# Linear attention and gated FFN on one core: the second batch's queries are loaded first, and later loads wait for transposes

## The chip, the cores and the metric

The kernel runs on one core of one Trainium2 chip, alone. The metric is the device time of one execution in microseconds. The kernel before took 594.44 us (median of 3 runs, 594.08 to 594.91). A core has five engines with a program each: TensorE (PE, matmuls), VectorE (DVE), ScalarE (ACT), GpSimd (POOL) and SyncE (SP). They meet only in semaphores. Here POOL issues all loads with a change of type, and SP issues the stores and the DMA transposes. The data itself is moved by 16 DMA engines, which both queues share.

## The reference

Eight batches of eight heads, 1024 positions, 64 numbers a head. Keys and values are projected along the positions to 64 rows, then comes softmax attention, then a feed-forward network with a sigmoid gate on all 8192 rows.

```python
k_proj = einsum('ks,bhsd->bhkd', E, k);  v_proj = einsum('ks,bhsd->bhkd', F, v)
attn = softmax(q @ k_proj^T / 8)               # over the 64 projected rows
x = (attn @ v_proj) as (8192, 512)             # heads side by side
out = (sigmoid(x @ w_gate) * (x @ w_val)) @ w_out      # 512 -> 1536 -> 512
```

Inputs and outputs are float32; the loads turn the inputs into bfloat16.

## The kernel before, in words

*Order.* Every instruction is entered in one list by hand (`add`), with the names of what it reads and writes. From the names the waits are worked out; each engine then runs its own instructions in the order of the list. A load or a transpose that waits therefore holds up what stands behind it on POOL or SP.

*Work.* A batch has two blocks of 512 rows. For a block, 12 slices of the hidden layer (`msteps`, slice m = 0 to 11) are computed: four matmuls each for gate and value, then the gate on ACT and DVE. Behind them come four output tiles of 128 rows (`oproj`, tt = 0 to 3), 12 matmuls each with the output weights wO, an evacuation by DVE into one of four buffers `ost` and a store from SP. The output tiles of a block stand among the slices of the following block. The list `todo` holds slices and tiles of a batch, numbered from 0; `gaps` says behind which slice a tile comes. For the first batch `todo` has 27 entries: 0 to 10 are block 0 (its first entry holds two slices), the rest block 1 with the tiles of block 0.

*Attention of the next batch.* Its steps are put between those entries (`put(i, fn)`: behind entry i; `spots` for the ten steps): `kv` projects keys and values (K first, then V), `turn_k` turns the keys, `sc(0)` and `sc(1)` compute the scores of heads 0 to 3 and 4 to 7, `den` and `split` compute the divisors (four reciprocals and two more operations on DVE), `bc(0)` and `bc(1)` broadcast them, `xo(0)` and `xo(1)` apply the values and write the FFN's input `xT`. The scores need queries with the head's 64 numbers on the partitions. For batch 0 TensorE turns them. From batch 1 on SP issues four DMA transposes of two heads each (`transpose_q`, r = 0 to 3, called r0 to r3), from the buffer `Qb` to `qT`. By the names that they write, r1 waits for r0 and r3 for r2. `sc(0)` reads r0 and r1, `sc(1)` r2 and r3.

*Loads.* K, V and Q of a batch are one load each. K and V go round three buffers `KV` (K of batch b in 2b mod 3, V in 2b+1 mod 3), Q has two. Called Kb, Vb and Qb with the batch's number, POOL's order before is: K0, half of Q0, V0, the gate and value weights and the other half of Q0 among them, K1, V1, Q1, then wO (which waits until Q1's transposes have finished), then K2, Q2, V2, K3, Q3, V3 and so on. A load waits until its buffer has been read. V2 goes where K1 was, V3 where K2 was: each V from batch 2 on waits for the `kv` of the batch before, and what stands behind it waits too.

*Transposes on SP.* Those of Q1 stand first behind the loads of E and F. Those of Q2 stand behind the store of output tile 0 of block 1, in batch 1. Those of batch b+2 stand at entry 20 of batch b, from b = 1 on.

Of the kernel before, what the change touches and what calls it, by code (L numbers as in the profile page):

```python
# [12 lines left out]
P = 128  # L13
# [14 lines left out]
class Plan:  # L28
# [9 lines left out]
    def add(self, eng, fn, r=(), w=(), x=(), dma=None):  # L38
        op = Op()
        op.eng, op.fn, op.dma, op.need = eng, fn, dma, False  # L40
        op.sem, op.val = None, 0
        deps = {}

        def dep(o, raw):
            if o is op:
                return
            if o.eng == eng and o.dma is None:
                if eng == "PE" or (eng != "POOL" and not raw):
                    return
            deps[id(o)] = o  # L50

        for k in r:
            for o in self.writers.get(k, ()):
                dep(o, True)
        for k in tuple(w) + tuple(x):
            for o in self.writers.get(k, ()):
                dep(o, False)
            for o in self.readers.get(k, ()):
                dep(o, False)
        for k in r:  # L60
            self.readers.setdefault(k, []).append(op)
        for k in tuple(w) + tuple(x):
            self.writers[k] = [op]
            self.readers[k] = []
        op.deps = list(deps.values())
        for o in op.deps:
            o.need = True
        if dma is not None:
            self.dma_count[dma] = self.dma_count.get(dma, 0) + 16
            op.sem, op.val = dma, self.dma_count[dma]  # L70
        self.ops.append(op)
        return op
# [46 lines left out]
def bass_linformer_attn__then__ffn_glu_sigmoid_kernel(  # L119
# [15 lines left out]
    NR = H // 2  # L135
    SCALE = 1.0 / (DH ** 0.5)

    with contextlib.ExitStack() as es:

        def sbuf(name, shape, dtype):  # L140
            return es.enter_context(nc.sbuf_tensor(name, shape, dtype))
# [31 lines left out]
        qT = [sbuf(f"qT{i}", [P, H, 512], BF16) for i in range(2)]  # L173
# [9 lines left out]
        wO = sbuf("wO", [P, NF, DM], BF16)  # L183
# [24 lines left out]
        def mm(b, o, lhsT, rhs, r, start=True, stop=True, tp=None, tr=False):  # L208
            kw = {}
            if tp is not None:  # L210
                kw["tile_position"] = tp
            if tr:
                kw["is_transpose"] = True
            else:
                kw["start"], kw["stop"] = start, stop
            return add("PE", lambda e: e.matmul(o, lhsT, rhs, **kw), r=r, x=[("bank", b)])  # L216
# [16 lines left out]
        def load(o, i, w, sem, r=()):  # L233
            add("POOL", lambda e: e.dma_start(o, i), r=r, w=w, dma=sem)  # L234

        def load_k(b):
            n = 2 * b % 3
            load(
                KV[n][:, :, :],
                k[b].rearrange("h (p t) d -> p h (t d)", t=NT),  # L240
                [("KV", n)],
                f"KV{n}",
            )

        def load_v(b):
            n = (2 * b + 1) % 3
            load(
                KV[n][:, :, :],
                v[b].rearrange("h (p t) d -> p h (t d)", t=NT),
                [("KV", n)],  # L250
                f"KV{n}",
            )

        def load_q(b):
            s = b % 2
            load(
                Qb[s][:, :, :],
                q[b].rearrange("h (p t) d -> p h (t d)", t=NT),
                [("Q", s, 0), ("Q", s, 1)],
                f"Q{s}",  # L260
            )
# [18 lines left out]
        def start_loads():  # L280
            for src, rows, n in ((E, slice(0, 64), "E"), (F, slice(64, 128), "F")):
# [4 lines left out]
                    dma="in" + n,  # L286
                )
            load_k(0)
            pool(lambda e: e.iota(col_i[:, :], [[1, P]], channel_multiplier=0), w=["col_i"])
            pool(lambda e: e.iota(row_i[:, :], [[1, 1]], channel_multiplier=1), w=["row_i"])  # L290
# [135 lines left out]
        def busy(n):  # L426
            for _ in range(n):
                mm(FB[3], bank[FB[3]][:, 0:P], ident[:, :], ident[:, :], ["ident"])
# [184 lines left out]
        def transpose_q(b):  # L613
            s = b % 2
            for r in range(NR):
                add(
                    "SP",
                    lambda e, r=r: e.dma_start_transpose(  # L618
                        qT[s][:, 2 * r : 2 * r + 2, :].rearrange("p h (t c) -> p (h t) c", c=P),
                        Qb[s][:, 2 * r : 2 * r + 2, :].rearrange("p h c -> p (h c)"),  # L620
                    ),
                    r=[("Q", s, 0), ("Q", s, 1)],
                    w=[("qT", s, r), ("qT", s, 0, r // 2), ("qT", s, 1, r // 2)],
                    dma=f"qT{s}{r}",
                )
# [130 lines left out]
        def msteps(blk, ms):  # L756
            s, hf = (blk // 2) % 2, blk % 2
            pbs = {}
            for m in ms:
                for n in "GV":  # L760
                    pbs[m, n] = ffn.next()
            for i in range(NI):
                for m in ms:
                    j = max(x for x in range(4) if WCH[x] <= m * P)
                    for n, W in (("G", wG), ("V", wV)):
                        if len(ms) > 1:
                            mm_one(blk, m, j, i, n, W, pbs[m, n], s, hf)
            if len(ms) == 1:
                m = ms[0]
                j = max(x for x in range(4) if WCH[x] <= m * P)  # L770
                for n, W in (("G", wG), ("V", wV)):
                    for i in range(NI):
                        mm_one(blk, m, j, i, n, W, pbs[m, n], s, hf)
            for m in ms:
                gate(blk, m, pbs[m, "G"], pbs[m, "V"])
# [81 lines left out]
        bc(1)  # L857
        xo(1)
        busy(10)
        load_k(1)  # L860
        load_v(1)
        load_q(1)

        def load_wo():
            load(
                wO[:, :, :],
                moe_w_out.rearrange("(m p) c -> p m c", p=P),
                ["wO"],
                "wO",
                r=[("qT", 1, r) for r in range(NR)],  # L870
            )

        for b in range(B):
            todo = []
            for blk in (2 * b, 2 * b + 1):
                ms = [[m] for m in range(NF)]
                if blk == 0:
                    ms = [[0, 1]] + ms[2:]
                if blk == 1:
                    gaps = {9: [0], 10: [1], 11: [2, 3]}  # L880
                else:
                    gaps = {2: [0], 5: [1], 8: [2], 11: [3]}
                for m in ms:
                    todo.append(lambda blk=blk, m=m: msteps(blk, m))
                    if blk >= 1:
                        for tt in gaps.get(m[-1], ()):
                            todo.append(lambda blk=blk, tt=tt: oproj(blk - 1, tt, ffn.next()))
            at = {}

            def put(i, fn):  # L890
                at.setdefault(i, []).append(fn)

            if b == 0:
                qt, sc, den, bc, xo = half_unit(1, att)
                put(1, lambda: (qt(0), qt(1)))
                put(2, lambda: sc(0))
                put(4, lambda: sc(1))
                put(5, den)
                put(7, lambda: (bc(0), xo(0)))
                put(9, lambda: (bc(1), xo(1)))  # L900
                spots = (14, 15, 17, 18, 19, 19, 21, 22, 23, 24)
            else:
                spots = (3, 6, 10, 13, 16, 16, 20, 23, 26, 29)
            if b + 1 < B:
                for i, fn in zip(spots, attention(b + 1)):
                    put(i, fn)
            def load_next(n):
                load_k(n)
                load_q(n)
                load_v(n)  # L910

            if b == 0:
                put(8, lambda: (transpose_q(1), load_wo()))
                put(22, lambda: load_next(2))
            else:
                if b == 1:
                    put(3, lambda: transpose_q(2))
                if b + 2 < B:
                    put(4, lambda b=b: load_next(b + 2))
                    put(20, lambda b=b: transpose_q(b + 2))  # L920
            for i, slot in enumerate(todo):
                slot()
                for fn in at.get(i, ()):
                    fn()
            assert max(at, default=0) < len(todo)
# [33 lines left out]
```

## Time and profile before

| | |
|---|---|
| median of 3 runs | 594.44 us |
| the profiled execution | 596.05 us, span 594.3 us |
| mean granted TensorE clock | 0.991 |
| PE busy | 563.1 us |
| DVE, ACT, POOL busy | 253.4, 200.8, 30.2 us |
| loads (queue q0), stores and transposes (queue q1) | 29.89 and 24.65 MB |

Times within the execution count from the start of the span. A row of a timeline or of the chain gives start and length in us, then engine, line and operation, then the tiles as written<-read with partitions and elements, and x with a count when several are merged. In brackets stands the idle time before it and what ended it. The granted clock is 1.00 at full speed and 0.50 at half. L216 is the line through which all matmuls are entered, L234 all loads, L618 the transposes, L681 to L691 the divisors. `pF` are the four PSUM banks of the FFN, `pA` those of attention. q0 and q1 are the DMA queues of POOL and SP.

### The profile page before, as it was taken

To read this page: it belongs to the slowest core of one execution; us is meant where nothing else is said; L and a number is where in the kernel's file an instruction comes from. 1 tells how busy PE (TensorE), PEld (TensorE's weight loads), DVE (VectorE), ACT (ScalarE), POOL (GpSimd) and SP (SyncE) were. 2 spreads that over 40 slices of the span, in tenths; PEclk is the share of its full clock that TensorE was granted. 3 is DMA by queue.
4 is the path that set the end of the run, shared out by engine and by line. 5 is a ranking of instruction groups with operands and counts; after the bars stand their busy time and mean duration, and the time that the engine had idled before them with its cause. 6 is when DMAs were issued, how large, how long until landed. Compare 5 with 4: busy or idle time off the path is not lost.

```text
span 594.3 us, 7808 instructions
## 1 busy us (share of the span) xinstructions
PE 563.1 (95%) x3150; PEld 255.5 (43%) x3206; DVE 253.4 (43%) x393; ACT 200.8 (34%) x371; POOL 30.2 (5%) x43
## 2 busy tenths in 40 slices
PE   5799859969999999999999999999999999999997
PEld 5444324424444444444444444444444444444443
DVE  2444425215363365433563364533654344633332
ACT  2454621323523533144423334234332434222220
POOL 8000300100001000010001000000000000000000
PEclk9999979989999999999999999999999999999999
DMA  9997699985405913095313904050331000000002
GB/s 155 202 206 134 93 203 233 165 135 107 106 37 97 169 54 88 19 169 114 72 54 69 206 29 106 36 104 21 54 88 37 19 35 36 18 36 36 35 36 88
DMA packets 70756, 55.04 MB, mean 93 GB/s; under 512 B 31168, under 2 KB 62400, under 8 KB 70720
## 3 DMA queue, kind: packets, MB, share of 16 engines
q0 software_dynamic: 31776, 29.89, 32.5%
q1 hardware_dynamic: 38944, 24.65, 15.6%
q8 instruction: 25, 0.41, 0.3%
q14 instruction: 11, 0.09, 0.0%
HBM read 60.29 MB, written 16.78 MB: 130 GB/s over the span
## 4 chain that ended last, share of the span: by engine, by line
PE 82%; DMA 16%; issue 1%; DVE 1%; SPq 0%; POOL 0%; POOLq 0%; DVEq 0%
PE pF L216 74%; PE pA L216 8%; DMA Qb<-in_q_dram 7%; DMA qT<-Qb 5%; DMA wO<-in_moe_w_out_dram 2%; DMA KV<-in_k_dram 2%; DVE xT L729 0%; DVE ost L822 0%; SPq L618 0%; POOL KV L234 0%; DVEq L102 0%; POOLq L102 0%; POOLq L944 0%; SPq L102 0%
## 5 line engine op out<-in xcount | busy, mean ns | idle before, releaser
L795 DVE SCALAR_TENSOR_TENSOR hT<-sig,pF 128x512 bf16<-128x512 f32 x192 | 131.2, 686 | 207.8 <-PE pF L216 135.2
L220 ACT ACTIVATE sig<-pF 128x512 f32<-128x512 f32 x192 | 115.3, 601 | 276.7 <-PE pF L216 269.2
L216 PE MATMUL pF<-xT,wG 128*128 128x512 bf16 x748 | 195.1, 380 | 2.3 <-issue 1.6
L216 PE MATMUL pF<-xT,wV 128*128 128x512 bf16 x748 | 195.1, 379 | 1.9 <-DVE xT L600 0.9
L216 PE MATMUL pF<-wO,hT 128*128 128x512 bf16 x705 | 165.9, 384 | 9.5 <-DMA wO<-in_moe_w_out_dram 8.0
L216 PEld LDWEIGHTS pF<-xT,wV 128*128 128x128 bf16 x768 | 75.1, 98 | 90.9 <-issue 0.6
L216 PEld LDWEIGHTS pF<-xT,wG 128*128 128x128 bf16 x768 | 71.1, 98 | 94.4 <-issue 15.1
L216 PEld LDWEIGHTS pF<-wO,hT 128*128 128x128 bf16 x720 | 69.4, 99 | 96.4 <-issue 8.9
L822 DVE TENSOR_SCALAR ost<-pF 128x512 f32<-128x512 f32 x60 | 41.5, 692 | 105.9 <-PE pF L216 105.9
L220 ACT ACTIVATE rb<-pA 128x512 f32<-128x512 f32 x62 | 32.2, 606 | 35.6 <-PE pA L216 35.6
L220 ACT ACTIVATE eT<-pA 128x512 bf16<-128x512 f32 x63 | 32.8, 606 | 13.9 <-PE pA L216 13.9
L729 DVE TENSOR_TENSOR xT<-pA,rb 128x512 bf16<-128x512 f32 x56 | 34.6, 679 | 0.0
L681 DVE RECIPROCAL rden<-pA 128x128 f32<-128x128 f32 x28 | 23.7, 908 | 0.0
L234 POOL DMA_DIRECT2D KV<-in_v_dram x8 | 7.1, 883 | 284.9 <-PE pA L216 284.9
L216 PE MATMUL pA<-qT,kpD 64*64 64x512 bf16 (+1 forms) x140 | 11.0, 374 | 5.8 <-DMA qT<-Qb 5.5
L220 ACT ACTIVATE kp<-pA 128x256 bf16<-128x256 f32 x8 | 3.1, 384 | 35.9 <-PE pA L216 35.9
L216 PE MATMUL pA<-KV,EFT 128*64 128x256 bf16 x240 | 14.6, 274 | 0.1
L216 PEld LDWEIGHTS pA<-KV,EFT 128*64 128x64 bf16 x240 | 12.5, 110 | 3.2 <-issue 3.0
L220 ACT ACTIVATE vpD<-pA 64x256 bf16<-64x256 f32 x28 | 10.5, 375 | 0.5
L216 PE MATMUL pA<-eT,vpD 64*64 64x512 bf16 (+1 forms) x136 | 10.4, 370 | 0.2 <-DVE xT L729 0.2
L216 PE MATMUL pA<-wO,hT 128*128 128x512 bf16 x47 | 10.5, 379 | 0.1
L234 POOL DMA_DIRECT2D Qb<-in_q_dram x9 | 8.1, 896 | 22.3 <-DMA qT<-Qb 22.2
(72 smaller groups left out, 114.0 us busy)
## 6 DMA issues: line engine op xcount, KB each, us to landing
out_dram<-ost SPq DMA_DIRECT2D x64, 256.0 KB, 2.0
KV<-in_k_dram POOLq DMA_DIRECT2D x8, 1024.0 KB, 16.0
KV<-in_v_dram POOLq DMA_DIRECT2D x8, 1024.0 KB, 11.8
Qb<-in_q_dram POOLq DMA_DIRECT2D x7, 1024.0 KB, 19.8
wO<-in_moe_w_out_dram POOLq DMA_DIRECT2D x1, 1536.0 KB, 12.1
Qb<-in_q_dram POOLq DMA_DIRECT2D x2, 512.0 KB, 16.4
wG<-in_moe_w_gate_dram POOLq DMA_DIRECT2D x2, 512.0 KB, 23.6
wV<-in_moe_w_val_dram POOLq DMA_DIRECT2D x2, 512.0 KB, 25.5
```

The source lines that it names most:

```text
L216: return add("PE", lambda e: e.matmul(o, lhsT, rhs, **kw), r=r, x=[("bank", b)])
L220: return add("ACT", lambda e: e.activation(o, i, func, scale=scale), r=r, w=w, x=x)
L234: add("POOL", lambda e: e.dma_start(o, i), r=r, w=w, dma=sem)
L681: lambda e, cc=cc: e.reciprocal(rden[:, cc], bank[bk][:, cc]),
L729: lambda e, r=r, g=g, n=n, bk=bks[g]: e.tensor_tensor(xT[s][:, r, :, 256 * g : 256 * g + 256], bank[bk][:, :].rearrange("p (f c) -> p f c" ...
L795: lambda e: e.scalar_tensor_tensor(hT[blk % 2][:, m, :], sg[:, :], 1.0, bank[pv][:, :], ALU.add, ALU.mult,),
L822: lambda e: e.tensor_scalar(o[:, :], bank[pb][:, :], 0.5, None, op0=ALU.mult),
```

## The change

1. Q1 is issued before K1 and V1. wO is issued right behind V1 and waits for nothing.
2. The load of K of batch b, for b of 2 and above, waits until all four transposes of the queries of batch b-1 have finished. Q and V of the batch stand behind it on POOL.
3. Q1's transposes move from entry 8 to entry 3 of batch 0; nothing else of SP stands between the two places. The loads of batch 2 move from entry 22 to entry 15. Q2's transposes move from entry 3 of batch 1 to entry 25 of batch 0, behind the store of output tile 2 of block 0.
4. In block 1 the output tiles of block 0 come behind slices 7, 9, 11 and 11, before behind 9, 10, 11 and 11. The attention steps of batch 1 from `sc(0)` on come one entry later.

```diff
+        def turned(b):
+            return [("qT", b % 2, r) for r in range(NR)]
+
         def load_k(b):
             n = 2 * b % 3
             load(
...
                 f"KV{n}",
+                r=turned(b - 1) if b >= 2 else (),
             )
...
         busy(10)
+        load_q(1)
         load_k(1)
         load_v(1)
-        load_q(1)
-
-        def load_wo():
-            load(
-                wO[:, :, :],
-                moe_w_out.rearrange("(m p) c -> p m c", p=P),
-                ["wO"],
-                "wO",
-                r=[("qT", 1, r) for r in range(NR)],
-            )
+
+        load(wO[:, :, :], moe_w_out.rearrange("(m p) c -> p m c", p=P), ["wO"], "wO")
...
                 if blk == 1:
-                    gaps = {9: [0], 10: [1], 11: [2, 3]}
+                    gaps = {7: [0], 9: [1], 11: [2, 3]}
...
-                spots = (14, 15, 17, 18, 19, 19, 21, 22, 23, 24)
+                spots = (14, 15, 18, 19, 20, 20, 22, 23, 24, 25)
...
             if b == 0:
-                put(8, lambda: (transpose_q(1), load_wo()))
-                put(22, lambda: load_next(2))
+                put(3, lambda: transpose_q(1))
+                put(15, lambda: load_next(2))
+                put(25, lambda: transpose_q(2))
             else:
-                if b == 1:
-                    put(3, lambda: transpose_q(2))
                 if b + 2 < B:
                     put(4, lambda b=b: load_next(b + 2))
                     put(20, lambda b=b: transpose_q(b + 2))
```

## The prediction

> **What bounds the kernel now.** I read the page first (busy times, then TensorE's 40 slices of 14.9 us, in tenths).
>
> ```profile
> PE 563.1 (95%) x3150; PEld 255.5 (43%) x3206; DVE 253.4 (43%) x393; ACT 200.8 (34%) x371; POOL 30.2 (5%) x43
> ...
> PE   5799859969999999999999999999999999999997
> ```
>
> TensorE is busy for 563.1 us, 95% of the span. From the tenth slice on (134 us) it is full; before that the first two slices (the first loads, which stay as they are) and the fifth, sixth and ninth are short. The view of waits (total, times, longest) names two DMA waits behind the latter three.
>
> ```profile
> PE pF L216 <- DMA wO<-in_moe_w_out_dram: 8.0, 1, 8.0
> PE pA L216 <- DMA qT<-Qb: 5.5, 2, 5.3
> ```
>
> So there is one wait of 8.0 us for the output weights and one of 5.3 us for transposed queries. The chain that ended last (start, length, what) tells why both come late.
>
> ```profile
> 15.08 39.64 DMA Qb<-in_q_dram
> 54.73 3.15 DMA qT<-Qb
> 57.90 1.24 SPq L618
> ...
> 68.05 12.13 DMA wO<-in_moe_w_out_dram
> 80.23 4.16 PE pF L216 x12
> ...
> 107.85 6.91 DMA qT<-Qb
> 114.77 12.80 DMA qT<-Qb
> ```
>
> Batch 1's queries are last in POOL's queue and land at 54.7; only when their four transposes are through is wO issued, at 68.05, and it lands at 80.2. Batch 2's transposes start at 107.85, beside loads, and the second takes 12.8 us where the first one at 54.73 took 3.15. TensorE's timeline gives the slots around the first place, the pace of an output tile, and the second place.
>
> ```profile
> 57.06 1.94 PE L216 MATMUL pA<-KV,EFT 128*64 128x256 bf16 x32
> ...
> 64.66 0.63 PE L216 MATMUL pA<-qT,kpD 64*64 64x512 bf16 x8
> 65.22 1.04 PE L216 MATMUL pF<-xT,wG 128*128 128x512 bf16 x4
> ```
> ```profile
> 114.00 2.76 PE L216 MATMUL pF<-wO,hT 128*128 128x512 bf16 x12
> 116.60 1.03 PE L216 MATMUL pF<-xT,wG 128*128 128x512 bf16 x4
> ```
> ```profile
> 121.88 0.41 PE L216 MATMUL pA<-qT,kpD 64*64 64x512 bf16 x4
> 127.62 0.64 PE L216 MATMUL pA<-qT,kpD 64*64 64x512 bf16 x4 [5.33 <-DMA qT<-Qb]
> 128.19 4.07 PE L216 MATMUL pF<-wO,hT 128*128 128x512 bf16 x12
> 132.10 1.03 PE L216 MATMUL pF<-xT,wG 128*128 128x512 bf16 x4
> 132.96 1.03 PE L216 MATMUL pF<-xT,wV 128*128 128x512 bf16 x4
> ```
>
> **What the two stalls cost in all.** Twelve wO matmuls take 2.60 us, start to next start (114.00 to 116.60). After the 5.3 us wait they take 3.91 (128.19 to 132.10), and the score matmuls before them 0.2 more than usual; after the 8.0 us wait they take 4.16. The windows say why (third figure from the end: granted clock).
>
> ```profile
> 76.00:78.00 2.00, 0.00 (x0) 0.00 (x0) 0.04 (x1) 0.00 (x0) 0.00 (x0) 0.57 1.24 207
> ...
> 126.00:128.00 2.00, 0.38 (x4) 0.14 (x4) 0.00 (x0) 0.00 (x0) 0.00 (x0) 0.87 1.16 115
> ```
>
> The first wait began at 72.25 (80.23 less 8.0) and the second at 122.3. A mean of 0.57 puts the drop to half clock at 76.3, and one of 0.87 at 127.5: 4.0 and 5.2 us into the waits. Each wait thus costs 1.5 us beyond its idle time: 9.5 and 6.8 us, 16.3 us together. More than that this change cannot bring.
>
> **The change, part by part.** *Queries first, wO without a wait.* POOL's load of Q1 takes K1's place, K1 takes V1's, V1 takes Q1's (V1 still waits until the first projection has read its buffer, the 1.36 us in the row of 14.21); wO comes right behind. The issue rows and those of landing (us from issue), K first, then V:
>
> ```profile
> 11.90 0.96 POOL L234 DMA_DIRECT2D KV<-in_k_dram  x1
> 14.21 0.88 POOL L234 DMA_DIRECT2D KV<-in_v_dram  x1 [1.36 <-PE pA L216]
> ```
> ```profile
> KV<-in_k_dram POOLq DMA_DIRECT2D x1, 1024.0 KB, 31.6
> ```
> ```profile
> KV<-in_v_dram POOLq DMA_DIRECT2D x1, 1024.0 KB, 35.5
> ```
>
> The three loads are of one size, so without other traffic Q1 lands at 43.5 (11.90 + 31.6), K1 at 49.7 and V1 at 54.7. The transposes of Q1 now start at 43.5, 11.2 us earlier, while K1, V1 and wO are still in flight. What sharing does is shown by the queue rows of three stretches: 44 to 46 (loads alone, 2 us), 121 to 122 (loads beside transposes, 1 us) and 112 to 113 (a load that has just started, 1 us). Columns are packets, MB, share.
>
> ```profile
> q0 software_dynamic: 403, 0.41, 123.4%
> ```
> ```profile
> q0 software_dynamic: 152, 0.16, 91.2%
> q1 hardware_dynamic: 152, 0.04, 29.4%
> ```
> ```profile
> q0 software_dynamic: 59, 0.06, 75.9%
> ```
>
> Loads alone move 0.205 MB/us; beside transposes 0.16, packet for packet. If all that is left after 43.5 runs at 0.16, the 9.2 us of data up to V1's end (43.5 to 52.7, two us before landing) become 11.8, so V1 lands between 54.7 and 57.3. Its projection is the second half of the 32 matmuls at 57.06, thus at 58.0: hidden, 0 us. wO is 1.57 MB: 7.7 us at the one rate, 9.8 at the other, so it lands between 62.4 and 67.1.
>
> *The slots in the second block.* Output tile 0 now follows slice 7, and both score steps are one slot later. No instruction is added; TensorE's order becomes slice 6, slice 7, scores 0, output tile 0, scores 1, slice 8, denominator. A slice is 1.73 (its halves start 0.86 apart, 132.10 and 132.96), eight score matmuls 0.56 (64.66 to 65.22). Scores 0 thus start at 66.4 and need transposes r0 and r1 (r1 at 66.7); tile 0 starts at 66.95 and needs wO: at most 0.2 us late, so I take 0. Scores 1 start at 69.55 and need r2, then r3 at 69.8.
>
> *The transposes beside loads.* r1 waits for r0, r3 for r2; r2 is issued when r1's issue ends, 1.24 us on (row of 57.90), and I let it land as much later. r0 takes 6.91 to 12.80 us beside loads, so it lands at 50.4 to 56.3, r1 at 57.3 to 69.1, r2 at 58.5 to 70.3, and r3, with the loads over, 3.15 later (row of 54.73), at 61.7 to 73.5. The fast end costs nothing; at the slow one r1 is 2.4 us late and r3, after that shift, 1.3: 3.7 us. Loads are in flight until about 65, so I lie nearer to the slow row, three quarters of the way: r1 at 66.2 in time, r3 at 70.8 and 1.0 us late. I take 1.0.
>
> *The reciprocals lose their cover.* VectorE has batch 1's divisor ready 5.64 us after the denominator starts (TensorE's row of 69.80; VectorE's row ends at 75.44).
>
> ```profile
> 69.80 0.61 PE L216 MATMUL pA<-eT,dsel 128*32 128x512 bf16 x8
> ```
> ```profile
> 74.69 0.75 DVE L691 SCALAR_TENSOR_TENSOR rhl<-rhi,negm,rden 128x512 bf16<-128x512 bf16 x1
> ```
>
> Until the broadcast needs it TensorE has the denominator (0.55), slice 9 (1.9 with gaps) and an output tile (2.60): 5.05. The wait for wO covered the rest before; now 0.6 us are late.
>
> *Batch 2's transposes earlier, later loads behind them.* They move from behind output tile 0 of the next block to behind tile 2 of this one; on SP they now stand ahead of tile 3's store, and every later store waits for them. The ring of four output tiles needs that store landed only four tiles later, over 20 us on, so 0 us. On POOL K2 waits for r3 at 71, and Q2 and V2 queue behind it. A load into an empty queue lands 9.9 us after its issue:
>
> ```profile
> Qb<-in_q_dram POOLq DMA_DIRECT2D x1, 1024.0 KB, 9.9
> ```
> ```profile
> 132.28 0.88 POOL L234 DMA_DIRECT2D Qb<-in_q_dram  x1 [22.23 <-DMA qT<-Qb]
> ```
>
> That is K2 at 81, Q2 at 86 and V2 at 91 (5.1 us each at 0.205 MB/us). The broadcast comes at 78.5 (69.55 + 0.56 + 1.73 + 1.0 + 5.64), and slices 10 and 11, tile 2 and the steps between take some 8 us more, so with tile 2's store the transposes start at about 88. Even at the pace of those of 107.85 (POOL's row of 132.28 waited for the last of the four: 24.4 us, with two loads beside them) they end at 112.4; the scores that waited at 122.3 come at about 113.9 now (121.88 - 9.5 + 1.6). The 5.3 us wait goes, with its clock: 6.8 us. K3, which waits for these transposes, and then V3 and Q3 are in place by 135 at the latest, and their projection comes only with the next batch. In the full slices nothing waits, and each later K merely moves behind transposes that had the engines to themselves.
>
> *Sum.* 594.44 - 16.3 + 1.0 + 0.6 = 579.7 us. The profiled execution took 596.05 us, 1.75 beyond its span and 1.6 above the median; I put the difference on the median.
>
> A page that bears on this: the Trainium skill (TensorE: Matmul & The Clock Gate, "Why this matters for your kernels") wants no idle gap above about 3 us between bursts of matmuls. The rows here kept full clock for 4.0 and 5.2 us. By the page the slow end of 3.7 us would cost 1.5 us more; by the rows it costs nothing, since its parts are 2.4 and 1.3 us with 2.6 us of matmuls between.
>
> **The rivals.**
> - *A slow first region.* The transposes and wO trail by several us, because one of the 16 engines lags: r0 above needed 6.91 us though the loads had barely begun. A 5 us wait in place of mine of 1.0, with its half clock, makes 579.7 + 4.0 + 1.5 = 585.2. Against it: wO has 4.5 us between its early landing and its slot.
> - *The second wait stays.* Q2 comes late behind K2, and the transposes meet V2 and the stores: 579.7 + 6.8 = 586.5. Against it: 1.5 us in hand even at the contended pace, and only r0 and r1 are needed first.
> - *Half clock after a short wait.* The waits of the slow end sit in one stretch of the clock's measure and halve it: 579.7 + 2.7 + 1.5 = 583.9. The two drops above speak against it.
> - *Slower: the loads crawl.* Loads ran at only 0.06 MB/us from 112 to 113, when a transpose had just passed. If that is what transposes do, wO's 1.57 MB takes 26 us after V1 at 57.3 and lands at 83, 16 us late; with r1 to r3 under it, half clock and the 0.6, 594.44 - 16.3 + 0.6 + 16.0 + 1.5 = 596.2. It decides from a wait for wO of 14.2 us, that is a landing at 81.2, at a mean of 0.066 MB/us. Against it: at 121 to 122, with transposes running, the rate was 0.16, and queues that start from empty are slow in any case.
>
> The new order surely reaches the chip, since queue order and waits are written out, so no rival stands for a change without effect; the waits could only move.
>
> **How the numbers follow.** Forecast 0.75 (579.7; its own range 577.9 to 582.6 from waits of 0 to 3.7 us and the divisor's wait of 0 to 0.8), slow first region 0.11, second wait 0.05, half clock 0.05, slower 0.04. The range of 577.9 to 586.5 takes in all but the last. What can be told from no change is 0.2%, 1.2 us. Every case but the slower one is far beyond it: faster 0.95, same 0.01, slower 0.04.
>
> **What would show it.** The wait of TensorE for wO is gone or below 1 us, with Q1 landed near 43.5, V1 by 57.3 and wO by 67; the clock stays 1.00 from 70 to 135; scores of batch 1 wait about 1 us for r3, and the broadcast about 0.6 us for the divisor; batch 2's transposes run from about 88 to 102, before V3 is issued. From the first FFN slice of batch 2 on all is as before, some 15 us earlier. It is wrong if V1 lands after 58, if wO lands after 70, if transposes beside three queued loads take more than 12.8 us, or if a wait above 4 us lets the clock fall.

## The result, and the profile after

The changed kernel takes 580.79 us (median of 4 runs, 579.87 to 581.52). The kernel before took 594.67 us beside it (594.08 to 595.89). The ratio is 0.9763 [0.9742, 0.9784]. The profiled execution took 581.52 us with a span of 579.7, 14.6 us shorter than the span before.

First the page's busy time, slices and granted clock, then the two rows of TensorE's waits that replace the pair shown of before (total, times, longest).

```profile
PE 559.1 (96%) x3150; PEld 253.9 (44%) x3206; DVE 253.3 (44%) x393; ACT 201.0 (35%) x371; POOL 30.3 (5%) x43
...
PE   5799899999999999999999999999999999999997
...
PEclk9999999999999999999999999999999999999999
```
```profile
PE pA L216 <- DMA qT<-Qb: 1.8, 1, 1.8
PE pA L216 <- DMA KV<-in_k_dram: 0.9, 1, 0.9
```

The three short slices are full and the clock stays whole. No wait for wO is left (the 0.9 belongs to the first projection of all). The 5.3 us wait for batch 2's queries is gone. The 1.8 us is a wait for batch 1's r3, and it has grown; before it was this:

```profile
67.62 0.41 PE L216 MATMUL pA<-qT,kpD 64*64 64x512 bf16 x4 [0.17 <-DMA qT<-Qb]
```

The chain after reads so:

```profile
11.89 31.74 DMA Qb<-in_q_dram
43.63 0.02 issue
43.64 12.16 DMA qT<-Qb
55.80 0.02 issue
55.82 1.24 SPq L622
57.06 0.04 issue
57.10 11.70 DMA qT<-Qb
68.81 0.02 issue
68.82 3.04 DMA qT<-Qb
```

Q1 lands at 43.6. Its transposes run from then to 71.9, beside the loads until wO has landed at 65.4 (four in 28 us; before, alone, in 13). TensorE's timeline shows what is still waited for, and that batch 2's scores come without a wait:

```profile
67.10 2.76 PE L216 MATMUL pF<-wO,hT 128*128 128x512 bf16 x11
69.80 0.41 PE L216 MATMUL pA<-qT,kpD 64*64 64x512 bf16 x4
72.00 0.41 PE L216 MATMUL pA<-qT,kpD 64*64 64x512 bf16 x4 [1.79 <-DMA qT<-Qb]
...
79.65 0.39 PE L216 MATMUL pA<-rhl,bsel 32*128 32x512 bf16 x4 [0.43 <-DVE rhl L695]
...
114.41 0.63 PE L216 MATMUL pA<-qT,kpD 64*64 64x512 bf16 x8
```

On SP batch 2's transposes are issued from 89.26 on, and POOL's K3 waits for them:

```profile
89.26 11.46 SPq L622 DMA_TRANSPOSE qT<-Qb  x4
```
```profile
103.40 0.89 POOL L234 DMA_DIRECT2D KV<-in_k_dram  x1 [28.20 <-PE pF L216]
```

The releaser in the last bracket is TensorE by name, but what POOL waited for is the last of those transposes, which landed then.

### The profile page after: what moved, and what is told of

It reads as the page before. It is cut to its first block, busy times and chain, and to the rows that moved or that the text cites. A ratio compares the mean times of both kernels' runs of the same rounds, so it can differ in the third digit from the quotient of the medians.

```text
span 579.7 us, 7813 instructions
## 1 busy us (share of the span) xinstructions
PE 559.1 (96%) x3150; PEld 253.9 (44%) x3206; DVE 253.3 (44%) x393; ACT 201.0 (35%) x371; POOL 30.3 (5%) x43
## 3 DMA queue, kind: packets, MB, share of 16 engines
q1 hardware_dynamic: 38944, 24.65, 16.5%
## 4 chain that ended last, share of the span: by engine, by line
PE 85%; DMA 10%; POOL 2%; DVE 1%; issue 1%; SPq 0%; POOLq 0%; DVEq 0%
PE pF L216 77%; PE pA L216 8%; DMA Qb<-in_q_dram 5%; DMA qT<-Qb 5%; DVE rden L685 1%; POOL wV L234 1%; POOL wG L234 1%; POOL KV L234 0%; POOL Qb L234 0%; SPq L622 0%; DVE rhl L695 0%; DVE ost L826 0%; DVE hT L799 0%; DVE rhi L693 0%; POOL pat_i L298 0%
## 5 line engine op out<-in xcount | busy, mean ns | idle before, releaser
L216 PE MATMUL pF<-wO,hT 128*128 128x512 bf16 x704 | 163.4, 379 | 1.6 <-issue 1.1
L220 ACT ACTIVATE eT<-pA 128x512 bf16<-128x512 f32 x63 | 32.8, 603 | 11.3 <-PE pA L216 11.3
L234 POOL DMA_DIRECT2D KV<-in_k_dram x8 | 7.2, 904 | 265.7 <-PE pF L216 208.6
L216 PE MATMUL pA<-KV,EFT 128*64 128x256 bf16 x240 | 14.6, 274 | 0.9 <-DMA KV<-in_k_dram 0.9
L216 PE MATMUL pA<-eT,vpD 64*64 64x512 bf16 (+1 forms) x136 | 10.4, 370 | 0.0
## 6 DMA issues: line engine op xcount, KB each, us to landing
wO<-in_moe_w_out_dram POOLq DMA_DIRECT2D x1, 1536.0 KB, 50.2
Qb<-in_q_dram POOLq DMA_DIRECT2D x2, 512.0 KB, 16.5
```

The source lines that it names most:

```text
L220: return add("ACT", lambda e: e.activation(o, i, func, scale=scale), r=r, w=w, x=x)
```

## The experiments

The theory under test says that the time follows from how long loads and transposes share the DMA engines, and from where each transfer lands against its slot. The rivals say that one part alone is the heart of it: queries first, the place of a transpose, the slots. Each kernel below is the changed one with the edit shown, unless said otherwise.

**The wait of the keys' loads, taken away (e1_no_gate).**

```diff
-                r=turned(b - 1) if b >= 2 else (),
+                r=(),
```

> The changed kernel, but no load of keys waits for transposes any more. Theory (sharing): what counts is how long loads share the 16 DMA engines with the transposes. K2 and Q2 then follow wO at once, the load queue stays full until about 78 us, the last transpose of batch 1 (71.9 us in the changed kernel) has to share too and lands near 81; scores 1 wait some 11 us instead of 1.8 and the clock halves: about 591 us. Rival (order alone): the gain comes from issuing Q1 first and wO without a wait, and the new waits of the keys' loads are idle caution: 580.8 us, as the changed kernel.

Measured: 597.34 us (595.78 to 599.28), ratio to before 1.0041 [1.0027, 1.0056]: slower than before, and 16.5 us slower than the changed kernel. In its chain r2 and then r3 read

```profile
56.14 17.52 DMA qT<-Qb
73.67 11.08 DMA qT<-Qb
```

and TensorE's timeline has

```profile
73.79 0.41 PE L216 MATMUL pA<-qT,kpD 64*64 64x512 bf16 x4 [3.31 <-DMA qT<-Qb]
84.89 0.64 PE L216 MATMUL pA<-qT,kpD 64*64 64x512 bf16 x4 [10.69 <-DMA qT<-Qb]
```

With K2 and Q2 behind wO, r2 takes 17.5 us and r3 11.1 instead of 3.0, and scores 1 wait 14.0 us in two pieces. The theory had the right cause but too little of it: 11 us of wait and 591 us. The rival falls: without the new waits the rest of the change makes the kernel slower.

**Batch 2's transposes: place and wait, a table of four (e2, e3, e4).** The fourth kernel is the changed one.

```diff
# e2_late_t2 and e4: back to the old place
-                put(25, lambda: transpose_q(2))
...
+                if b == 1:
+                    put(3, lambda: transpose_q(2))
```
```diff
# e3_gate_k2 and e4: only K2 waits
-                r=turned(b - 1) if b >= 2 else (),
+                r=turned(b - 1) if b == 2 else (),
```

> The changed kernel, but batch 2's transposes stand where they stood before, behind output tile 0 of the next block. Theory (sharing): they start near 100 us instead of 89, still ahead of K3, which waits for them, so they run alone and end near 112, before their scores at 114.4: about 580.8 us, no wait. Rival (place): the second wait went because the transposes start earlier; put back they are late again: about 587.6 us.

> The changed kernel, but only K2 waits for transposes, K3 and later keys do not. K3 and Q3 then follow V2 from 75 us on, V3 and K4 follow the projection at 101, and batch 2's transposes (from 89) share the engines all along. Theory (sharing): r0 near 101, r1 near 111, r2 near 114, r3 near 120, against scores at 114.4 and 120.9: the early place has room for that, 581 us, at most 583. Rival (the waits of later keys are what removes the second wait): it is back, 586 us or more.

> Both taken back: only K2 waits, and batch 2's transposes stand in their old place (start near 100 us). Theory (sharing): beside Q3, V3 and K4, r0 lands near 111 and r1 near 120 against a need at 114.7: 5 to 6 us of wait, and half clock for a while: about 587.5 us. If early place and waits were no substitutes for each other, this would be the sum of what the two kernels with one of them taken back lose.

| | K3 and later wait | only K2 waits |
|---|---|---|
| new place (entry 25) | 580.79 (changed kernel) | 583.65 (583.39 to 584.94) |
| old place | 580.74 (580.41 to 580.98) | 592.45 (588.36 to 593.52) |

The place alone brings nothing once the loads wait (e2). With both taken back TensorE stands still for

```profile
123.77 0.64 PE L216 MATMUL pA<-qT,kpD 64*64 64x512 bf16 x4 [9.35 <-DMA qT<-Qb]
```

and with the place alone for

```profile
118.07 0.41 PE L216 MATMUL pA<-qT,kpD 64*64 64x512 bf16 x4 [0.99 <-DMA qT<-Qb]
```

So each of the two replaces nearly all of the other: taken back alone they lose nothing and 2.9 us, together 11.7. Of e3's 2.9 us this profile shows 1.0 in the second place; the execution also lost some 3 us in start-up (below). Two other executions of e3 kept a mean clock of 1.000 and still took 583.39 and 583.58, so the start-up is not the whole of it; how their waits split stays open. The wait in e4 was 9.4 us where I had 5 to 6, since r0 and r1 needed 11.9 us each beside the loads. Three of e4's ten executions took only 588.4 to 589.8; why is not shown.

e1 takes away the wait of K2 and those of the later keys, e3 only the latter. The difference between them, 597.34 against 583.65, puts 13.7 us on K2's wait.

**Queries last again (e5_q_last).**

```diff
-        load_q(1)
         load_k(1)
         load_v(1)
+        load_q(1)
```

> The changed kernel, but the load order of batch 1 is K1, V1, Q1 again; wO still follows at once without a wait. Theory (sharing): Q1 lands at 54.7 instead of 43.6, but its transposes then share the engines with wO alone: r0 near 64.5, the others without sharing at 68, 69.5 and 72.8, against needs at 66.8 and 70.1: 2.7 us of wait instead of 1.8, about 581.7 us. Rival (queries first is the heart of the change): transposes that start 11 us later end 11 us later, near 83; scores 1 wait over 10 us and the clock falls: 592 us.

Measured: 580.79 us (580.48 to 582.32), the same as the changed kernel. The chain:

```profile
15.05 39.03 DMA Qb<-in_q_dram
54.08 0.02 issue
54.09 9.23 DMA qT<-Qb
63.33 0.02 issue
63.34 1.24 SPq L622
64.59 0.04 issue
64.63 3.15 DMA qT<-Qb
67.78 0.02 issue
67.79 3.04 DMA qT<-Qb
```

The transposes start 10.4 us later and end at 70.8, 1.0 earlier than in the changed kernel: only r0 shares the engines with wO, the rest run alone. The wait for r3 is 0.9 us, where 2.7 were expected. What a start ahead of the loads wins is lost again by sharing. The rival, and the change's own title, fall here.

**wO waits again (e6_wo_waits).**

```diff
-        load(wO[:, :, :], moe_w_out.rearrange("(m p) c -> p m c", p=P), ["wO"], "wO")
+        def load_wo():
+            load(wO[:, :, :], moe_w_out.rearrange("(m p) c -> p m c", p=P), ["wO"], "wO", r=turned(1))
...
-                put(3, lambda: transpose_q(1))
+                put(3, lambda: (transpose_q(1), load_wo()))
```

> The changed kernel, but wO waits for the transposes of Q1 again, as in the kernel before; queries stay first. Theory (sharing): the transposes share with K1 and V1 only and end near 64, then wO needs 12.1 us and lands near 76; output tile 0 (due at 67.1) waits 9 us and the clock halves, the 1.8 us for r3 go: about 589.5 us. Rival (queries first alone removes the first wait, since the transposes end earlier): about 581 us.

Measured: 592.19 us (590.06 to 594.01), 11.4 us above the changed kernel.

```profile
78.94 1.03 PE L216 MATMUL pF<-wO,hT 128*128 128x512 bf16 x2 [11.28 <-DMA wO<-in_moe_w_out_dram]
```

The wait was 11.3 us where I had 9: wO was issued at 65.4, not 64, and took 13.5 us, not 12.1. Of the first half of the change (load order, wO without a wait, slots), wO without a wait is the part that counts most.

**The slots (e7_old_slots, e11_old_slots_filled).**

```diff
-                    gaps = {7: [0], 9: [1], 11: [2, 3]}
+                    gaps = {9: [0], 10: [1], 11: [2, 3]}
...
-                spots = (14, 15, 18, 19, 20, 20, 22, 23, 24, 25)
+                spots = (14, 15, 17, 18, 19, 19, 21, 22, 23, 24)
```

> The changed kernel, but tiles and attention steps stand in their old slots. Theory: the scores are due one slot earlier while the transposes land as in the changed kernel (r1 65.8, r2 68.8, r3 71.9): 0.8 us of wait at scores 0, 3.6 at scores 1 instead of 1.8 in all: about 583.4 us. Rival (the new slots matter nothing, or cost by the divisor's wait): 580.8 us or less.

Measured: 584.09 us (583.25 to 585.8). The number is near the theory's, but the profile is not: no wait for queries in it. The execution lost some 3 us at half clock between 20 and 32 us, so its scores came late enough to find the transposes landed. That the number agrees is luck. So the pair had to be tried with a start-up that keeps its clock, by filler matmuls whose result nobody reads:

```diff
# e12_filled and e11: fillers in the start-up, at seven places
         keep_k(bk, 0)
+        busy(7)
         turn_k(whole)
+        busy(10)
...
+        busy(6)
         sc(0)
+        busy(3)
         sc(1)
+        busy(12)
         den()
+        busy(8)
...
-        busy(10)
+        busy(22)
```

> The changed kernel with 58 more of the small filler matmuls in the start-up of batch 0 (some 3 us of TensorE, put where it waits), all to a bank that nobody reads. Profiles of several kernels here lose up to 3 us between 15 and 32 us, when the clock halves though no wait is above 2 us. Theory (the clock follows the busy share of a stretch, and start-up is near its limit, so that chance decides): with the filler no execution loses its clock there, 580.5 us with all executions within 1 us. Rival (the half clock there has another cause): the filler costs time, 581.5 us or more, and slow start-ups stay.

> The kernel with old slots and the same 58 fillers, which takes the start-up's clock out of the comparison. Theory: scores are due one slot earlier than in the changed kernel, so about 4.4 us of wait for r1 to r3 instead of 1.8, with the clock perhaps still whole: 583.3 us. Rival (what the old slots lost was the start-up's clock alone): as the changed kernel with fillers, 580.5 us.

Measured: 579.81 us (579.27 to 580.16) with the new slots and 582.76 us (581.84 to 583.65) with the old ones. In the latter

```profile
65.16 0.41 PE L216 MATMUL pA<-qT,kpD 64*64 64x512 bf16 x4 [0.37 <-DMA qT<-Qb]
69.74 0.41 PE L216 MATMUL pA<-qT,kpD 64*64 64x512 bf16 x4 [1.99 <-DMA qT<-Qb]
```

are 2.4 us, and in the former the view of waits has none for queries. The slots are worth 2.9 us.

**Transposes without the chain (e8_unchained), and all together (e10_best).**

```diff
-                    w=[("qT", s, r), ("qT", s, 0, r // 2), ("qT", s, 1, r // 2)],
+                    w=[("qT", s, r)],
...
-                                ["kpD", ("qT", s, hf, R)],
+                                ["kpD", ("qT", s, hf, R), ("qT", s, 2 * R), ("qT", s, 2 * R + 1)],
```

> The changed kernel, but the four transposes of a batch no longer wait for each other (r1 for r0, r3 for r2): all four are issued in a row, and the scores of batch 0 carry the names that order the buffer's reuse. Theory (sharing, and some 3.5 us without a packet at the start of each link of the chain): the four end near 69.5 instead of 71.9, so the wait of 1.8 us goes; wO loses the stretches in which it ran alone and lands near 67.3, against 67.1: about 579.3 us. Rival (the chain keeps transposes out of the loads' way): wO lands several us late and tile 0 waits: 582 us or more.

> The changed kernel with three edits: load order K1, V1, Q1; transposes not chained; the 58 fillers. Theory: transposes start near 54, share with wO until about 64 and end near 68, wO lands near 65, so neither is waited for; only the divisor's wait of about 0.9 us is left: 579.6 us. Rival (each edit has already taken what there is to take): 580.6 us, as the changed kernel.

Measured: e8 580.56 us (580.0 to 583.41), e10 (e8's edit, queries last and the fillers) 580.52 us (579.43 to 580.7). Both wait no longer for r3. In e8 wO is 0.17 us late, as expected, but what follows moves up:

```profile
67.19 2.76 PE L216 MATMUL pF<-wO,hT 128*128 128x512 bf16 x11 [0.17 <-DMA wO<-in_moe_w_out_dram]
...
78.27 0.40 PE L216 MATMUL pA<-rhl,bsel 32*128 32x512 bf16 x4 [0.95 <-DVE rhl L695]
```

The divisor is now 0.95 us late instead of 0.43. Of the 1.8 us won, 0.7 go to wO and to the divisor; the 1.1 that should remain do not stand out of the spread. e10 confirms neither its forecast of 579.6 nor an advantage over the fillers alone. The lowest of all is e12, the changed kernel with fillers, ratio to before 0.9723 [0.9693, 0.9754]: 1.0 us below the changed kernel in the median, with overlapping intervals. This 1.0 us is not shown to come from the clock, since all four executions of the changed kernel had a mean clock of 1.000 too. What e12's profile lacks is the wait for r3; why its transposes ended earlier stays open.

**The second half alone (e9_second_only),** made from the kernel before:

```diff
+                r=turned(b - 1) if b >= 2 else (),
...
+                put(25, lambda: transpose_q(2))
...
-                if b == 1:
-                    put(3, lambda: transpose_q(2))
```

> The kernel before with only the second half of the change: K of batch 2 and later waits for the preceding batch's transposes, and batch 2's transposes stand at entry 25. Load order of batch 1, wO's wait and all slots are as before. Theory: the first wait stays at 8.0 us with its half clock; batch 2's transposes start near 97, when V2 has landed, run alone and end near 109, before their scores: 5.3 + 1.5 us go, about 587.7 us. Rival (the halves help only together, since loads and transposes are shifted by the first stall): 594 us.

Measured: 587.58 us (586.94 to 588.53), ratio 0.986 [0.9822, 0.9897]. No wait for queries is left in the second place. The total is the theory's, but in part by luck: the kernel before took 596.21 us beside it, so the gain is 8.6 us and not 6.8, and the first wait did not stay at 8.0:

```profile
77.93 4.45 PE L216 MATMUL pF<-wO,hT 128*128 128x512 bf16 x12 [4.70 <-DMA wO<-in_moe_w_out_dram]
```

Here Q1's transposes started at 53.5 and wO was issued at 65.7, where before it was 54.7 and 68.05. The two halves do not add up simply: e9, the second half alone, gains 1.4%, e4, the first half with K2's wait, 0.6% (the wait in the second place is longer there), both 2.4%.

## Why the prediction was right

- *Total.* 579.7 forecast, 580.79 measured. The medians fell by 13.9 us against 14.7 forecast; the spans of the two profiled executions, both slower than their medians, by 14.6. With the measured 1.79 and 0.43 us in place of 1.0 and 0.6 the sum gives 580.4.
- *What the two stalls cost.* 8.0 and 5.3 us with 1.5 us of half clock each. After the change both are gone and the clock is whole. TensorE's busy time fell by 4.0 us; 3.0 were forecast as the half clock's cost, and where the other 1.0 lies is not shown.
- *Landing of the loads.* V1 was put between 54.7 and 57.3 and wO between 62.4 and 67.1. The rows after (us from issue) give 43.6 for Q1, 50.2 for K1, 56.4 for V1 and 65.4 for wO, which were issued at 11.89, 12.76, 14.35 and 15.22:

```profile
wO<-in_moe_w_out_dram POOLq DMA_DIRECT2D x1, 1536.0 KB, 50.2
Qb<-in_q_dram POOLq DMA_DIRECT2D x1, 1024.0 KB, 31.7
KV<-in_k_dram POOLq DMA_DIRECT2D x1, 1024.0 KB, 37.4
KV<-in_v_dram POOLq DMA_DIRECT2D x1, 1024.0 KB, 42.1
```

- *Sharing packet for packet.* From 52 to 53 us the two queues read as at 121 to 122 before, and loads fall to the same 0.16 MB/us:

```profile
q0 software_dynamic: 155, 0.16, 93.0%
q1 hardware_dynamic: 154, 0.04, 29.8%
```

- *Transposes beside loads.* 1.0 us was taken and 1.79 measured. The term was too small: r3 landed at 71.9, not at 70.8, since r2 (the row of 57.10) ended only at 68.8. Three quarters of the way from 61.7 to 73.5 is in fact 70.55, 0.75 us late, so the working gave even less than the 1.0 that was taken. Nor is 12.8 us the slow end that the prediction took it for: in e1, with K2 and Q2 queued behind the three loads, one needed 17.5.
- *The divisor.* 0.6 us forecast, 0.43 measured. The wait for r3 covers part of it: in the profiles with such a wait of 0.9 us or more (changed kernel, e1, e2, e4, e5, e11) the divisor is 0.43 or 0.44 us late, in those with none (e3, e6, e7, e8, e10) 0.95.
- *Batch 2's transposes.* Forecast from 88 to 102, measured from 89.3 to 103.4, no wait: right. But I gave the new place and the loads' waits one account; e2 and e3 show that either does most of it.
- *What the sum did not ask.* The sum has no term for the keys' waits; the prediction works out when K2 lands with its wait, and not what happens without it. Against the order before it changes little (K2 issued at 69.05 before, at 72.57 now), but e1 shows what the waits prevent: 16.5 us, of which 13.7 are K2's. And queries first, the first item of the change, is worth 0 (e5). The sum was right, but it did not say which part carries it: taken back alone, wO without a wait costs 11.4 us and the new slots 2.9, and without the keys' waits none of the gain is left.
- *The rivals.* The slow first region needed a 5 us wait and got 1.8. The crawling loads did not appear. The second wait would have stayed with neither wait nor place (e4). Half clock after a short wait did not occur where I had put it, but it does occur in start-up. The 1.5 us more that the prediction prices "by the page" for the slow end takes two gaps of 2.4 and 1.3 us, with matmuls between, for one of 3.7.

## What to carry to other kernels

Before moving a transfer earlier, ask what it will share the engines with: a start 10 us earlier beside three loads ended no sooner than a late start beside the last of them. A wait that keeps later bulk loads out of the way of short transfers somebody needs soon can be worth more than any reordering; here the one edit that looks like caution decided between 2.4% faster and 0.4% slower. And test parts one by one even when the sum is right, since two parts may replace each other and a third may carry nothing.

## What the runs showed of the hardware that I had not expected

*A transpose under load starts late.* Alone, the one issued at 54.73 before landed after 3.15 us in all. In the changed kernel the one issued at 43.64 left q1's row empty until after 47: from 46 to 47 only loads moved.

```profile
q0 software_dynamic: 199, 0.20, 121.0%
```

Nearly 4 us pass before its first packet, and about as long again after r1's issue at 55.8 (none until 59.5). So each of these two links of the chain costs that, beside the shared packets. Why the start is late is not shown.

*The clock can fall without a long wait.* In e3's start-up, between 12 and 32 us, TensorE waits at most 1.44 us at a time, yet it is at half clock from 20.4 us on, by the 0.59 below (windows of e3, second figure: TensorE's busy time in 2 us; third from the end: clock):

```profile
18.00:20.00 2.00, 1.29 (x14) 0.67 (x12) 0.39 (x1) 1.12 (x3) 0.00 (x0) 1.00 1.33 196
20.00:22.00 2.00, 0.99 (x10) 0.85 (x12) 1.14 (x3) 0.00 (x0) 0.00 (x0) 0.59 1.45 196
22.00:24.00 2.00, 2.00 (x22) 1.35 (x20) 0.85 (x2) 0.75 (x2) 0.00 (x0) 0.50 1.45 195
```

In the changed kernel the same stretch has 1.59 and 1.52 and keeps its clock:

```profile
18.00:20.00 2.00, 1.59 (x16) 0.89 (x16) 0.06 (x1) 1.45 (x3) 0.00 (x0) 1.00 1.31 194
20.00:22.00 2.00, 1.52 (x24) 1.24 (x24) 1.86 (x4) 0.40 (x2) 0.00 (x0) 1.00 1.45 196
```

But it also kept its clock through an emptier stretch just before, so the busy time of a window does not decide alone:

```profile
12.00:14.00 2.00, 1.06 (x16) 0.80 (x16) 0.00 (x0) 0.16 (x1) 1.73 (x2) 1.00 1.43 199
14.00:16.00 2.00, 1.04 (x20) 0.89 (x21) 0.00 (x0) 0.82 (x2) 1.65 (x2) 1.00 1.27 207
```

With e3, half clock until some 31 us costs about 3 us. Of the eleven profiles without fillers six show half clock somewhere between 15 and 32 us (e1, e3, e4, e6, e7, e9) and five do not; of the three with fillers (e10, e11, e12) none does. In e12 TensorE is busy for at least 1.9 of every 2 us from 12 to 24, and none of its four times is above 580.16. That the fillers prevent the half clock is likely by this count, but three profiles do not show it. The Trainium skill (TensorE: Matmul & The Clock Gate, Part 1) lets the clock follow how busy the array was in a free-running stretch of about 3.4 us. The rows above are compatible with that, if chance decides where such a stretch begins, but no run here shows the stretch or a limit. The advice on the same page of the Trainium skill to avoid gaps above about 3 us does not cover a stretch that is busy by half in many short pieces. Before, two single gaps kept full clock for 4.0 and 5.2 us.
